# Windowed attention and a gated FFN: the first FFN products tile by tile, q and k transposed on TensorE up to tile 12, five load buffers and twelve V tiles

## The chip, the cores and the metric

The kernel runs on one core of a Trainium2 chip. Its time is device microseconds of one execution; the time before is the median of seven runs. The profiled execution is one of them, and all times inside the kernel are microseconds from the first instruction of its trace.

## The reference

Attention over a sliding window of 128 keys with a distance bias for each head, then an FFN with a SiLU gate on all tokens. Batch 8, 8 heads, 576 positions, head size 64; so 4608 tokens of width 512, and an inner width of 1536. All inputs and the output are float32.

```python
scores = q @ k.T / sqrt(64)
rel = pos[:, None] - pos[None, :]
bias = -slope[h] * abs(rel)                # slope[h] = 2 ** -(h + 1)
scores = where((rel >= 0) & (rel < 128), scores + bias, -1e9)
attn = softmax(scores)                     # its sum plus 1e-9 below
x = (attn @ v).transpose(0, 2, 1, 3).reshape(4608, 512)
g, val = x @ w_gate, x @ w_val
out = (g * sigmoid(g) * val) @ w_out
```

## The kernel before

**Tiles.** Two batches make a super-group of nine ranks: four tiles of 128 positions of each batch, and a ninth that holds the last 64 positions of both. There are 36 ranks and 36 attention units, one for each rank of queries. A unit p needs k of its rank and q of its own and the next rank; the units 3, 7 and 8 of a super-group use blocks of 128 queries and a combined mask.

**An attention unit.** GpSimd's queue loads q, k and v of a rank and casts them to float16 (`load_qk`, L174; `load_v`, L168). q and k go into `nat` buffers, four of each; v goes into a ring of `NV` = 14 tiles. q and k must be transposed: for ranks below `QK_DMA_FROM` = 9 on TensorE (`transposed`, L201), followed by a copy out of PSUM (q by VectorE at L206, k by ScalarE at L204, in the first four ranks all by VectorE); from rank 9 on by a DMA transpose that SP issues (`transpose`, L222). `scores` makes k times q on TensorE (L254, L282), exp on ScalarE (L259, L286) and the product with the distance mask on VectorE (L263, L290). `weighted` multiplies by v (L314), and VectorE divides by the sums (L316, L317). `x_transposed` turns x so that the FFN can use it: on TensorE with a ScalarE copy (L340, L341), from unit 24 on by DMA.

**The FFN.** Tokens form nine blocks of 512 columns; the ninth block collects the eight odd tiles of 64. `gate_val` makes, for each of the twelve row groups m, the gate product and the value product (`wide`, L363: four matmuls of 128 x 512 each), tanh on ScalarE (L374), `uu` on VectorE (L376) and `hT` on VectorE (L380). Block 0 and block 8 are multiplied by w_out in a plain way (`project`, L393); blocks 1 to 7 with seven products of half size in Strassen's manner (`strassen`, L472 to L502), whose steps are put between the next block's products at the places in `AT`.

**The first four units.** `first_tiles` runs them before the FFN, in an order written out by hand. TensorE starts with `WARM` = 7 matmuls on zeros. `REPEAT` says how often each early transpose is done, so that TensorE has something to do; only the last writes what is used. `need[i]` is the number of transposes that unit i wants. After unit 3's weighted product, the products of m = 0, 1 and 2 of block 0 are made for 384 columns (three tiles), and `wide` keeps the half-filled bank in `early`; `gate_val` adds the last 128 columns when tile 3 is transposed.

**PSUM.** `ps_f` has three banks "gv" and one "po"; `ps_a` has four banks "a" that scores, transposes and others take in turn. `OTHER` names the products of block 0 that use an "a" bank instead of a "gv" bank.

**The order.** In `first_tiles` and in the first `ALONE` = 8 half steps of the FFN (that is, m = 0 to 3), TensorE, VectorE and ScalarE keep the order of the code. After that a planner orders each engine's queue, with priorities from the order in which the code is written; SP's and GpSimd's queues are the planner's from the start. The main loop advances attention by a target that grows with the FFN's steps. `ahead` writes DMA transposes up to four units before they are needed, but stops at the first rank below `QK_DMA_FROM`. `loads_to(i + 7)` keeps the loads seven ranks ahead. Every engine works through its queue in order.

**Weights.** `load_w` brings column slices of the gate and value weights: 128 columns of each, then the next 384, then twice 512, between the loads of q, k and v. w_out comes in two halves after tile 8.

Of the kernel before, what the change touches and what calls it, by code (L numbers as in the profile page):

```python
# [15 lines left out]

P = 128
WIN = 128
QK_DMA_FROM = 9
X_DMA_FROM = 24  # L20
ALONE = 8
MANUAL = "compute"
# [1 line left out]
ENGINES = {"all": None, "compute": {ET.PE, ET.DVE, ET.Activation}, "pe": {ET.PE}}  # L24
WARM = 7
IDLE = {("k", 0): 0, ("q", 0): 2}
REPEAT = {("q", 1): 4, ("k", 1): 4, ("q", 2): 3}
FIRST = 4
LEAD = 6
PRE = 0  # L30
# [4 lines left out]
def slot(h):  # L35

    return 4 * (h // 4) + 2 * (h % 2) + (h % 4) // 2
# [9 lines left out]
def kernel(  # L47
# [10 lines left out]
    nc = tc.nc  # L58
# [21 lines left out]
    idm = consts.tile([P, P], FP16, name="idm")  # L80
    nc.scalar.dma_start(idm, idm_d.ap())

    idm2 = consts.tile([P, P], FP16, name="idm2")
# [14 lines left out]
    idle = kT[:, NK - 1].rearrange("p j t -> p (j t)")  # L98
# [19 lines left out]
    wv2 = moe_w_val.rearrange("(kb p) f -> p kb f", p=P)  # L118
    wo2 = moe_w_out.rearrange("(a p) d -> p a d", p=P)

    nat = ctx.enter_context(tc.tile_pool(name="nat", bufs=4))
    epool = ctx.enter_context(tc.tile_pool(name="ep", bufs=3))
    xpool = ctx.enter_context(tc.tile_pool(name="xp", bufs=3))
    bpool = ctx.enter_context(tc.tile_pool(name="bp", bufs=3))
# [9 lines left out]
        for _ in range(n):  # L134
            nc.tensor.matmul(t_, idle[:, 0:P], idle, start=True, stop=True)

    NV = 14
    va_all = []
    for n in range(NV // 2):
        tv = consts.tile([P, 2, H, D + 1], FP16, name=f"va{n}")  # L140
# [15 lines left out]
    def source(src, rank):  # L156

        s, c = divmod(rank, 9)
        if c == 8:
            return [((64 * n, 64 * n + 64),  # L160
                     src[2 * s + n, :, 512:576, :].rearrange("h p d -> p h d")) for n in range(2)]
        b, t = 2 * s + c // 4, c % 4
        return [((0, P), src[b, :, t * P:(t + 1) * P, :].rearrange("h p d -> p h d"))]

    def load_v(rank):
        va[rank] = va_all[rank % NV]
        for (p0, p1), src in source(v, rank):
            nc.gpsimd.dma_start(va[rank][p0:p1, :, 0:D], src)  # L168
# [8 lines left out]
    def load(rank):  # L177
        load_qk(rank)
        load_v(rank)

    def transposed(name, rank):

        if rank < FIRST:
            pt = ps_f.tile([P, 4, P], FP32 if (name, rank) in hw else FP16, name="pt",
                           tag="gv" if name == "k" else "po", bufs=3 if name == "k" else 1)
        else:
            pt = ps_a.tile([P, 4, P], FP16, name="pt", tag="a")
        if (name, rank) in hw:

            for _ in range(IDLE[(name, rank)]):  # L190
                nc.tensor.matmul(pt.rearrange("p j t -> p (j t)"), idle[:, 0:P], idle,
                                 start=True, stop=True)
            for j in range(4):
                nc.tensor.transpose(pt[:, j, :], hw[(name, rank)][:, j * P:(j + 1) * P], idf)
            nc.vector.tensor_copy(transposed_home(name, rank), pt)
            return
        t_ = (natk if name == "k" else natq).pop(rank)

        for _ in range(REPEAT.get((name, rank), 2) if rank < FIRST else 1):
            for j in range(4):  # L200
                nc.tensor.transpose(pt[:, j, :], t_[:, 2 * j:2 * j + 2, :],  # L201
                                    idm if rank < FIRST else idm2)
        if name == "k" and rank >= FIRST:
            nc.scalar.copy(transposed_home(name, rank), pt)  # L204
        else:
            nc.vector.tensor_copy(transposed_home(name, rank), pt)  # L206
# [9 lines left out]
    def transpose(n):  # L216
        name, rank = order[n]
        if rank < QK_DMA_FROM:
            transposed(name, rank)
# [74 lines left out]
    def weighted(i):  # L294

        s, p = units[i]
        x = xpool.tile([P, H, D], FP16, name="x", tag="x")
        xs[i] = x
        for half in range(2):
            pool, tag = (ps_f, "gv") if i < FIRST else (ps_a, "a")  # L300
            av = pool.tile([P, 4, D + 1], FP32, name="av", tag=tag)
            todo = []
            for j in range(4):
                h = 4 * half + j
                if p == 8:
                    for n, kt in enumerate((3, 7, 8)):
                        todo.append((j, ex[(s, "c", n)][:, slot(h), :], va[9 * s + kt][:, h, :]))
                else:
                    if p not in (0, 4):
                        todo.append((j, ex[(s, p - 1)][:, slot(h), 128:256],  # L310
                                     va[9 * s + p - 1][:, h, :]))
                    todo.append((j, ex[(s, p)][:, slot(h), 0:128], va[9 * s + p][:, h, :]))
            for n, (j, w, val) in enumerate(todo):
                nc.tensor.matmul(av[:, j, :], w, val, start=(n == 0), stop=(n == len(todo) - 1))  # L314
            rec = xpool.tile([P, 4, 1], FP32, name="rec", tag="rec", bufs=4)
            nc.vector.reciprocal(rec, av[:, :, D:D + 1])  # L316
            nc.vector.tensor_mul(x[:, 4 * half:4 * half + 4, :], av[:, :, 0:D],  # L317
                                 rec.broadcast_to([P, 4, D]))
# [31 lines left out]
    hT = {}  # L350

    early = {}
    OTHER = {(0, 1, "v"), (0, 2, "g"), (0, 2, "v")}

    def wide(n, m, which, c1=512):

        w, ms = wg_sb if which == "g" else wv_sb, slice(m * P, (m + 1) * P)
        ps, c0 = early.pop((n, m, which), (None, 0))
        if ps is None:
            pool, tag = (ps_a, "a") if (n, m, which) in OTHER else (ps_f, "gv")  # L360
            ps = pool.tile([P, 512], FP32, name="p" + which, tag=tag)
        for kb in range(NKB):
            nc.tensor.matmul(ps[:, c0:c1], w[:, kb, ms], xT[n][:, kb, c0:c1],  # L363
                             start=(kb == 0 and c0 == 0), stop=(kb == NKB - 1 and c1 == 512))
        if c1 < 512:
            early[(n, m, which)] = (ps, c1)
        return ps
# [136 lines left out]

    AT = {*range(2, 9), *range(10, 17)}

    def ffn():

        for n in range(NBLK):
# [6 lines left out]
            for m in range(NMB):  # L518
                for half, _ in enumerate(gate_val(n, m)):
                    yield 1.0  # L520
                    if n > 1 and 2 * m + half in AT:
                        next(parts)
# [25 lines left out]
    def transposes_to(n):  # L548
        nonlocal done_t
        while done_t < n:  # L550
            transpose(done_t)
            done_t += 1

    def ahead(i):

        n = need[min(i + 4, last)]
        while done_t < n and order[done_t][1] < loaded and order[done_t][1] >= QK_DMA_FROM:
            transposes_to(done_t + 1)

    def run(steps):  # L560
        for fs in steps:
            for f in fs:
                f()
            yield

    def first_tiles():

        first_masks()
        transposes_to(need[0] + 1)
        for n, _ in enumerate(run(scores(0))):  # L570
            if n == 2:
                transposes_to(need[1])
        for i in range(FIRST):
            if i + 1 < FIRST:
                for n, _ in enumerate(run(scores(i + 1))):
                    if n == 0 and i + 2 < FIRST:
                        transposes_to(need[i + 2])
            weighted(i)
            if i > 0:
                x_transposed(i - 1)  # L580

        for m, which in ((0, "g"), (0, "v"), (1, "g")):
            wide(0, m, which, 384)
        x_transposed(FIRST - 1)
        for m, which in ((1, "v"), (2, "g"), (2, "v")):
            wide(0, m, which, 384)

    def attention():

# [17 lines left out]
    def load_w(c0, c1):  # L607
        for src, dst in ((wg2, wg_sb), (wv2, wv_sb)):
            nc.gpsimd.dma_start(dst[:, :, c0:c1], src[:, :, c0:c1])
# [8 lines left out]
    load_qk(3, "k")  # L618
    load_v(2)
    load_v(3)  # L620
    load_w(0, 128)
    load_w(128, 512)
    load(4)
    load_qk(5, "q")
    load_w(512, 1024)
# [29 lines left out]
    def everything():  # L655
        nonlocal done
        base = 0
        busy(WARM)
        with tc.manual_schedule(engines=ENGINES[MANUAL]):
            first_tiles()  # L660
            done = FIRST
            steps = progress(ffn())
            while (at := next(steps)) < ALONE:
                if at == 4.0:
                    make_masks()
                if at == 6.0:
                    nc.scalar.copy(idm2, idm)
        for step in steps:

            b1 = 24 + 3 * PRE  # L670

            lead = LEAD if done < X_DMA_FROM - 2 else LEAD + 4
            blk = (0 if step + LEAD < b1 else 1 if step + LEAD < 60
                   else min(NBLK - 1, 2 + int((step + lead - 60) // 34.5)))
            if step < b1:

                target = base + max(0, step - ALONE) + max(0, step - 16) * (32 - b1 + ALONE) / (b1 - 16)
            elif step < 60:
                target = base + 32 + SECOND * 8 * (step - b1) / (60 - b1)
            else:  # L680
                target = base + 32 + SECOND * 8 + (step - 60) * RATE * 8 / 34.5
            while (n_att < target or done < ready[blk]) and att_step():
                pass
# [32 lines left out]
```

## Time and profile before

| what | value |
|---|---|
| median of 7 runs | 360.1 us (358.19 to 362.95) |
| the profiled execution | 359.31 us |
| its span, first to last instruction | 357.5 us |
| TensorE busy | 340.0 us |
| VectorE busy | 271.2 us |
| ScalarE busy | 177.6 us |
| mean granted TensorE clock | 0.999 |
| DMA transposes, qT and kT | 27 and 27 |
| packets of GpSimd's DMA queue | 116224, 18.62 MB |
| packets of SP's and ScalarE's DMA queue | 43232, 18.49 MB |

The span is what lies between the first and the last instruction of the trace; the time of the same execution is 1.8 us more. In a row of a timeline the first number is the start, the second the length, then come engine, line, operation, what is written from what, the shape and the count; the bracket holds the idle time of the engine before it and what ended that. Matmuls that follow each other overlap, so that the length of a group is less than its count times the length of one. A digit in a row of slices is the busy share of one fortieth of the span (8.9 us), in tenths.

### The profile page before, as it was taken

The page shows a single profiled execution, that of the slowest core. Times are in us where ns is not written, and L with a number is a line of the kernel's source. Part 1 is how long each engine was busy: PE and PEld are TensorE (multiplying, and loading weights), DVE is VectorE, ACT ScalarE, POOL GpSimd, SP SyncE. Part 2 cuts the span into 40 slices and gives each one's busy share as a digit, 9 for nine tenths or more (in the row PEclk, how much of TensorE's full clock was granted, in tenths as well). Part 3 has the DMA queues.
Part 4 walks back from the last instruction along what each step waited for, and adds up shares of the span by engine and source line. Part 5 has one row for each costly group of instructions (what it writes and reads, how often), then busy time and mean ns, then how long its engine had stood idle before and what let it go on. Part 6 is the DMA issues. An engine that isn't in the chain of part 4 may idle for free.

```text
span 357.5 us, 7133 instructions
## 1 busy us (share of the span) xinstructions
PE 340.0 (95%) x2701; PEld 193.6 (54%) x2701; DVE 271.2 (76%) x594; ACT 177.6 (50%) x351; POOL 106.7 (30%) x132
## 2 busy tenths in 40 slices
PE   7788997999999999999999999999999999999995
PEld 4554453444456655565466655564665566456543
DVE  4748974997887699768987998789877955975540
ACT  4737684455655455556565454555454323333321
POOL 8954662574926355556420001000000000000000
PEclk9999999999999999999999999999999999999999
DMA  9999999999999999999992213202021201101104
GB/s 150 170 186 187 167 175 95 133 118 160 131 152 153 146 162 175 178 154 162 176 143 87 41 67 32 85 20 75 15 76 29 75 2 59 60 2 60 60 17 102
DMA packets 159939, 37.87 MB, mean 106 GB/s; under 512 B 150432, under 2 KB 155424, under 8 KB 159904
## 3 DMA queue, kind: packets, MB, share of 16 engines
q0 software_dynamic: 116224, 18.62, 81.5%
q1 hardware_dynamic: 43232, 18.49, 28.5%
q8 instruction: 21, 0.34, 0.4%
q10 hardware_dynamic: 448, 0.30, 0.3%
q14 instruction: 14, 0.11, 0.1%
HBM read 37.91 MB, written 9.44 MB: 132 GB/s over the span
## 4 chain that ended last, share of the span: by engine, by line
PE 69%; DMA 15%; DVE 7%; POOL 4%; ACT 3%; issue 2%; ACTq 0%; POOLq 0%; SPq 0%; DVEq 0%
PE pg L363 21%; PE pv L363 20%; PE po L472 15%; DMA wv_sb<-in_moe_w_val_dram 6%; DMA qT<-qn 3%; PE av L314 3%; PE ps L254 3%; DMA wo_sb<-in_moe_w_out_dram 3%; PE po L393 2%; DMA qn<-in_q_dram 2%; PE p L472 2%; DVE uu L376 2%; DVE hT L380 1%; POOL va L168 1%; ACT exc L286 1%
## 5 line engine op out<-in xcount | busy, mean ns | idle before, releaser
L374 ACT ACTIVATE tt<-pg 128x512 f16<-128x512 f32 x108 | 64.9, 603 | 109.6 <-PE pg L363 103.6
L363 PE MATMUL pg<-xT,wg_sb 128*128 128x512 f16 (+2 forms) x444 | 115.4, 374 | 1.0 <-ACT xT L341 0.7
L363 PE MATMUL pv<-xT,wv_sb 128*128 128x512 f16 (+2 forms) x444 | 113.1, 373 | 1.2 <-DVE uu L376 1.2
L376 DVE SCALAR_TENSOR_TENSOR uu<-tt,pg 128x512 f16<-128x512 f16 x107 | 73.0, 683 | 37.8 <-ACT tt L374 37.4
L380 DVE TENSOR_TENSOR hT<-uu,pv 128x512 f16<-128x512 f16 x108 | 73.7, 682 | 6.0 <-PE pv L363 2.7
L363 PEld LDWEIGHTS <-wg_sb 128*128 128x128 f16 x444 | 41.5, 98 | 38.0 <-issue 3.5
L363 PEld LDWEIGHTS <-wv_sb 128*128 128x128 f16 x444 | 41.2, 98 | 38.5 <-issue 4.9
L259 ACT ACTIVATE ex<-ps 128x512 f16<-128x512 f32 x96 | 50.0, 610 | 9.5 <-PE ps L254 9.4
L168 POOL DMA_DIRECT2D va<-in_v_dram x40 | 34.4, 869 | 42.7 <-PE av L314 32.2
L174 POOL DMA_DIRECT2D qn<-in_q_dram x39 | 33.8, 871 | 34.9 <-DMA qT<-qn 21.5
L174 POOL DMA_DIRECT2D kn<-in_k_dram x39 | 33.5, 865 | 29.6 <-DMA kT<-kn 24.4
L472 PEld LDWEIGHTS <-hT 128*128 128x128 f16 x336 | 32.1, 98 | 14.9 <-issue 1.2
L263 DVE TENSOR_TENSOR ex<-ex,m_reg 128x1024 f16<-128x1024 f16 x48 | 32.8, 686 | 8.5 <-ACT ex L259 8.3
L472 PEld LDWEIGHTS <-S 128*128 128x128 f16 x252 | 23.9, 98 | 12.7 <-issue 4.1
L317 DVE TENSOR_TENSOR x<-av,rec 128x256 f16<-128x256 f32 x72 | 28.6, 420 | 0.4
L286 ACT ACTIVATE exc<-psc 128x512 f16<-128x512 f32 x40 | 21.0, 604 | 5.7 <-PE psc L282 5.7
L472 PE MATMUL po<-T,hT 128*128 128x256 f16 x168 | 22.9, 272 | 0.1
L472 PE MATMUL po<-T,S 128*128 128x256 f16 x168 | 22.9, 273 | 0.0
L314 PE MATMUL av<-va,ex 128*128 128x65 f16 x384 | 20.7, 193 | 2.2 <-DVE x L317 1.3
L314 PEld LDWEIGHTS <-ex 128*128 128x128 f16 x384 | 18.1, 97 | 6.3 <-DVE x L317 2.0
L254 PE MATMUL ps<-qT,kT 64*128 64x256 f16 x192 | 18.0, 272 | 3.6 <-DMA qT<-qn 2.1
L393 PE MATMUL po<-wo_sb,hT 128*128 128x512 f16 x84 | 19.7, 379 | 0.0
(72 smaller groups left out, 278.7 us busy)
## 6 DMA issues: line engine op xcount, KB each, us to landing
out_dram<-osb SPq DMA_DIRECT2D x32, 256.0 KB, 3.0
va<-in_v_dram POOLq DMA_DIRECT2D x32, 128.0 KB, 7.9
qn<-in_q_dram POOLq DMA_DIRECT2D x31, 128.0 KB, 8.1
kn<-in_k_dram POOLq DMA_DIRECT2D x31, 128.0 KB, 8.0
wo_sb<-in_moe_w_out_dram POOLq DMA_DIRECT2D x2, 768.0 KB, 9.9
wg_sb<-in_moe_w_gate_dram POOLq DMA_DIRECT2D x2, 512.0 KB, 10.6
wv_sb<-in_moe_w_val_dram POOLq DMA_DIRECT2D x2, 512.0 KB, 12.3
out_dram<-osb SPq DMA_DIRECT2D x6, 128.0 KB, 2.3
```

The lines of the kernel that those rows point to most:

```text
L168: nc.gpsimd.dma_start(va[rank][p0:p1, :, 0:D], src)
L174: nc.gpsimd.dma_start(t_[p0:p1], src)
L254: nc.tensor.matmul(two[par][:, j, :], kT[rows, ks, pair, :], qT[rows, p:p + 2, pair, :], start=(j == 0), stop=(j == 1))
L259: nc.scalar.activation(e[:, o:o + 2, :], banks[q4][par], AF.Exp, scale=scale)
L263: nc.vector.tensor_mul(e[:, o, :], e[:, o, :], reg[:, o, :])
L314: nc.tensor.matmul(av[:, j, :], w, val, start=(n == 0), stop=(n == len(todo) - 1))
L317: nc.vector.tensor_mul(x[:, 4 * half:4 * half + 4, :], av[:, :, 0:D], rec.broadcast_to([P, 4, D]))
L363: nc.tensor.matmul(ps[:, c0:c1], w[:, kb, ms], xT[n][:, kb, c0:c1], start=(kb == 0 and c0 == 0), stop=(kb == NKB - 1 and c1 == 512))
L374: nc.scalar.activation(tt, pg, AF.Tanh, scale=0.5)
L376: nc.vector.scalar_tensor_tensor(out=uu, in0=tt, scalar=one if (n, m) == PIN else 1.0, in1=pg, op0=ALU.add, op1=ALU.mult)
L380: nc.vector.tensor_mul(hT[n][:, m, :], uu, pv)
L472: nc.tensor.matmul(dst, a[:, m, cols], b[:, m, :], start=(start and m == 0), stop=(m == HM - 1), skip_group_check=True)
```

## The change

- `QK_DMA_FROM` goes from 9 to 13: q and k of ranks 9 to 12 are transposed on TensorE, with the copies that belong to it.
- `nat` has five buffers for q and five for k instead of four; the ring of V has twelve tiles instead of fourteen.
- The first slice of the gate and value weights is 256 columns instead of 128, the second 256 instead of 384.
- `begin` makes products of block 0 for the tiles that are there: those of m = 0 and 1 for one tile in unit 2 and for the second in unit 3; those of m = 2 for two tiles after that; then the third tile for all. `OTHER` now names the four products of m = 0 and 1, so those of m = 2 use "gv" banks.
- In the units 1 to 3 each half of `weighted` begins with two matmuls of 256 columns on zeros.
- `REPEAT`: k of rank 1 two instead of four times, q of rank 2 four instead of three times. q of rank 2 is transposed one step earlier in the code, ahead of unit 0's mask products.
- The copy of the identity (`idm2`) and the four mask copies move to other half steps of the FFN, and the steps of Strassen's products to other places in `AT` (the same number of places).

```diff
--- before.py
+++ after.py
@@ -16,7 +16,7 @@
 
 P = 128
 WIN = 128
-QK_DMA_FROM = 9
+QK_DMA_FROM = 13
 X_DMA_FROM = 24
 ALONE = 8
 MANUAL = "compute"
@@ -24,7 +24,7 @@
 ENGINES = {"all": None, "compute": {ET.PE, ET.DVE, ET.Activation}, "pe": {ET.PE}}
 WARM = 7
 IDLE = {("k", 0): 0, ("q", 0): 2}
-REPEAT = {("q", 1): 4, ("k", 1): 4, ("q", 2): 3}
+REPEAT = {("q", 1): 4, ("k", 1): 2, ("q", 2): 4}
 FIRST = 4
 LEAD = 6
 PRE = 0
@@ -118,7 +118,7 @@
     wv2 = moe_w_val.rearrange("(kb p) f -> p kb f", p=P)
     wo2 = moe_w_out.rearrange("(a p) d -> p a d", p=P)
 
-    nat = ctx.enter_context(tc.tile_pool(name="nat", bufs=4))
+    nat = ctx.enter_context(tc.tile_pool(name="nat", bufs=5))
     epool = ctx.enter_context(tc.tile_pool(name="ep", bufs=3))
     xpool = ctx.enter_context(tc.tile_pool(name="xp", bufs=3))
     bpool = ctx.enter_context(tc.tile_pool(name="bp", bufs=3))
@@ -134,7 +134,7 @@
         for _ in range(n):
             nc.tensor.matmul(t_, idle[:, 0:P], idle, start=True, stop=True)
 
-    NV = 14
+    NV = 12
     va_all = []
     for n in range(NV // 2):
         tv = consts.tile([P, 2, H, D + 1], FP16, name=f"va{n}")
@@ -299,6 +299,11 @@
         for half in range(2):
             pool, tag = (ps_f, "gv") if i < FIRST else (ps_a, "a")
             av = pool.tile([P, 4, D + 1], FP32, name="av", tag=tag)
+            if 0 < i < FIRST:
+
+                for _ in range(2):
+                    nc.tensor.matmul(av.rearrange("p j d -> p (j d)")[:, 0:256], idle[:, 0:P],
+                                     idle[:, 0:256], start=True, stop=True)
             todo = []
             for j in range(4):
                 h = 4 * half + j
@@ -350,7 +355,7 @@
     hT = {}
 
     early = {}
-    OTHER = {(0, 1, "v"), (0, 2, "g"), (0, 2, "v")}
+    OTHER = {(0, 0, "g"), (0, 0, "v"), (0, 1, "g"), (0, 1, "v")}
 
     def wide(n, m, which, c1=512):
 
@@ -504,7 +509,7 @@
 
 
 
-    AT = {*range(2, 9), *range(10, 17)}
+    AT = {2, 3, *range(5, 10), *range(11, 18)}
 
     def ffn():
 
@@ -563,12 +568,18 @@
                 f()
             yield
 
+    def begin(n, tiles):
+
+        for m, which in ((0, "g"), (0, "v"), (1, "g"), (1, "v"), (2, "g"), (2, "v"))[:n]:
+            if early.get((0, m, which), (None, 0))[1] < tiles * P:
+                wide(0, m, which, tiles * P)
+
     def first_tiles():
 
         first_masks()
         transposes_to(need[0] + 1)
         for n, _ in enumerate(run(scores(0))):
-            if n == 2:
+            if n == 0:
                 transposes_to(need[1])
         for i in range(FIRST):
             if i + 1 < FIRST:
@@ -576,14 +587,15 @@
                     if n == 0 and i + 2 < FIRST:
                         transposes_to(need[i + 2])
             weighted(i)
+
+            if i >= 2:
+                begin(4, i - 1)
             if i > 0:
                 x_transposed(i - 1)
-
-        for m, which in ((0, "g"), (0, "v"), (1, "g")):
-            wide(0, m, which, 384)
+        begin(6, 2)
+        begin(4, 3)
         x_transposed(FIRST - 1)
-        for m, which in ((1, "v"), (2, "g"), (2, "v")):
-            wide(0, m, which, 384)
+        begin(6, 3)
 
     def attention():
 
@@ -618,8 +630,8 @@
     load_qk(3, "k")
     load_v(2)
     load_v(3)
-    load_w(0, 128)
-    load_w(128, 512)
+    load_w(0, 256)
+    load_w(256, 512)
     load(4)
     load_qk(5, "q")
     load_w(512, 1024)
@@ -661,10 +673,10 @@
             done = FIRST
             steps = progress(ffn())
             while (at := next(steps)) < ALONE:
-                if at == 4.0:
+                if at == 2.0:
+                    nc.scalar.copy(idm2, idm)
+                if at == 5.0:
                     make_masks()
-                if at == 6.0:
-                    nc.scalar.copy(idm2, idm)
         for step in steps:
 
             b1 = 24 + 3 * PRE
```

## The prediction

> **What bounds the kernel.** I read the page first: busy shares, then the slices.
>
> ```profile
> PE 340.0 (95%) x2701; PEld 193.6 (54%) x2701; DVE 271.2 (76%) x594; ACT 177.6 (50%) x351; POOL 106.7 (30%) x132
> PE   7788997999999999999999999999999999999995
> PEclk9999999999999999999999999999999999999999
> DMA  9999999999999999999992213202021201101104
> ```
>
> TensorE is busy 340.0 of 357.5 us, its clock is full in every slice, and its free time lies in the first seven slices (some 62 us) and the last. So the next view is TensorE's timeline for those 62 us. In each row the bracket is the idle time before the work and what ended it:
>
> ```profile
> 11.85 0.61 PE L254 MATMUL ps<-qT,kT 64*128 64x256 f16 x8 [1.24 <-DVE qT L206]
> ...
> 21.57 0.81 PE L363 MATMUL pg<-xT,wg_sb 128*128 128x384 f16 x4 [0.67 <-ACT xT L341]
> ...
> 25.69 0.39 PE L363 MATMUL pg<-xT,wg_sb 128*128 128x128 f16 x4
> ...
> 30.35 0.38 PE L201 MATMUL pt<-idm,kn 128*128 128x128 f16 x4
> 30.57 0.61 PE L201 MATMUL pt<-idm,qn 128*128 128x128 f16 x8
> 32.14 1.02 PE L363 MATMUL pv<-xT,wv_sb 128*128 128x512 f16 x4 [0.96 <-DVE uu L376]
> ...
> 60.90 0.27 PE L254 MATMUL ps<-qT,kT 64*128 64x256 f16 x1 [2.06 <-DMA qT<-qn]
> ```
>
> Adding the idle rows from 11.85 to 60.90 gives 8.1 us; after 61 us the idle rows over 0.15 us add to only 2.2. After 61 us, then, an instruction added to TensorE costs its full time, and a faster other engine brings nothing. Before 61 us, VectorE's and the loads' timelines say what TensorE waits for:
>
> ```profile
> 10.76 0.69 DVE L263 TENSOR_TENSOR ex<-ex,m_reg 128x1024 f16<-128x1024 f16 x1 [1.01 <-ACT ex L259]
> 11.37 0.42 DVE L206 COPY qT<-pt 128x512 f16<-128x512 f16 x1
> ...
> 48.30 0.88 POOL L174 DMA_DIRECT2D qn<-in_q_dram  x1
> 49.20 2.62 POOL L168 DMA_DIRECT2D va<-in_v_dram  x3
> 60.41 0.88 POOL L174 DMA_DIRECT2D qn<-in_q_dram  x1 [8.59 <-DMA kT<-kn]
> ```
>
> From 13.2 to 20 us the windows view gives VectorE 6.61 busy of 6.80: it is the bound there. The last fence shows GpSimd's load queue standing 8.59 us behind a DMA transpose. Over the span the DMA slices say 9 at 95 GB/s around there (slice 6 of the page) against 175 a slice earlier: the transposes fill the DMA engines without moving much.
>
> **Start to 13 us.** k of tile 1 is transposed twice instead of four times, q of tile 2 four times instead of three. A 128-column transpose takes 219 ns alone, but four end within 0.38 us, so one more costs 0.056. Eight fewer take 0.45 us off before tile 0's products (at 9.22), which then wait for the copy of q1 (ends 8.85): 0.3 gained. That copy of q2 (L206) is now ahead of the first mask product in VectorE's order. Products 8.9 to 9.45, sixteen transposes of 1.06 us (the row at 7.34), copy 10.5 to 10.9, and tile 1's products start at 10.95 instead of 11.85. VectorE's chain from 13 us on hangs on these, so it moves 0.9 us earlier and its last weighted tile ends near 20.75 instead of 21.64.
>
> **FFN products in slices.** Before, the six products of m = 0 to 2 wait until three tiles are there (21.57), and their last 128 columns start at 25.69. After, four of them take tiles 0 and 1 into the gaps of the weighted stage. From VectorE at 20.75: the transposes of tile 2's x sit behind the second slice (16 matmuls, 0.88 us), so they start near 20.8; start to copied xT took 1.2 us (20.31 to 21.51), so xT is there at 22.0; third slices 0.88, tile 3's transposes at 22.9, its xT at 24.0, with m = 2's slices between. Last columns from 24.0: **1.7 us earlier**. The twelve extra matmuls on zeros (256 columns, half of the 0.217 spacing of the 512 rows: 1.3 us) stand where TensorE waits for VectorE; without that cover they would cost 1.3, and I take 0.
>
> A rule speaks against slicing. The Trainium skill, "TensorE: Matmul & The Clock Gate", section "Back-to-back issue gap", gives about 81 ns per matmul of 128 columns in a stream of weight loads and matmuls. Eighty such and eight of 256 columns would be 7.3 us; by the rows here (0.056 and 0.108) 5.3, against 5.25 for the 24 of 384 (0.162) and 24 of 128 before. By the page the slices lose 2 us and eat the gain; the rows of this trace cover the same shape with its weight loads, so I take 0.1.
>
> **Halved W slices.** The first pieces, 128 columns, were issued at 10.05 and 10.79 and landed 5.3 and 5.0 us later; the 384-column ones, issued at 11.52 and 12.25, landed at 18.6 and 20.5, 1.9 us apart for 384 KB. Two of 256 KB first should land near 16.1 and 17.4. They are wanted at about 17.8, so a wait lies between 0 and 0.5; I take 0. The total bytes are unchanged.
>
> **Banks of m = 2 to 4.** m = 2's products now take two of the three "gv" banks, so m3's value product waits for the uu of m2. VectorE's series of uu and hT, 0.6 us apart, starts 1.7 us earlier (25.0), so m2's uu ends near 28.1; TensorE stands from 26.2 to 28.1. Then come m3's value product, twelve transposes (0.66), and m4: its value product starts near 30.6 against 32.14. So the 0.96 us wait goes, one of 1.9 comes instead, and **1.5 to 1.6** of the lead is left. The mask copies move behind m2's tanh (2.3 us on ScalarE), hidden by VectorE's series; the idm2 copy (0.3) too.
>
> **Five load buffers.** At 38.23 tile 8's k load waits 0.39 us for a k buffer, and wo's first half goes ahead of it. With five it can go first; wo's piece took 3.0 us of landing (44.2 to 47.2), so tile 8 lands up to 3 us earlier. That lets the lead survive to 58.8 us, where block 0's output products end. If not, the lead waits for tile 8's data (nearest 0, at most 1.6 lost). Twelve V tiles instead of fourteen: V of tile 12 goes out at 50.9 onto tile 0's place, free since 15 us; later ones are early by tens of us. I take 0.
>
> **Tiles 9 to 12 on TensorE.** Eight transposes times four matmuls times 0.056 is **1.8 us** added, and 8 copies (four of 0.59 on ScalarE, four of 0.42 on VectorE, which has 2.9 us free of 20 between 60 and 80): hidden, up to 1.7 if VectorE has no room. Removed: the **2.06 us** wait at 60.90. q of tile 10 landed at 56.4 (48.30 + 8.1), its DMA transpose only at 60.8. By TensorE it is ready at 56.4 + 0.22 + 0.42 and some 0.3 of handing over, 57.3; TensorE gets there at 58.84 - 1.6 + three transposes 0.66, about 57.9. So the wait goes whole. The Trainium skill speaks against moving transposes here too (same page, "Part 4: PE-mode transpose"): about 275 ns each in one kernel. 32 of them would be 8.8 us, and the change would lose 5; the rows (0.38 for four, running on from each other) make it 1.8, and they decide.
>
> The moved Strassen places (one slot later) change no count; the four waits of 0.3 to 0.4 on L476 may move: within 0.5 either way, 0 taken.
>
> **Sum.** -1.6 - 2.06 + 1.8 = -1.9 us. The profiled execution took 359.31 (span 357.5 and 1.8 around it), so 357.4; it lies 0.8 below the median of 360.1, so the median becomes **358.2**. A measurement of this kernel can tell about 1% (3.6 us) from no change.
>
> **Rivals.** (a) *The wait moves.* DMA transposes now begin at tile 13, and only after tile 12's are written, so its k and q get one tile of lead; the old rank-9 wait (2.06) can reappear near 92 us, where tile 13 follows tile 12 within 3 us. Or tile 8's data holds the early lead back. Either takes about 2: 360.3. For: the DMA slices stay at 9. Against: the load queue no longer stands 8.6 us behind transposes.
> (b) *More of the idle time goes.* If the new bank wait doesn't come (VectorE ahead) and the waits for x at 43 to 54 us go (0.7), and those at 27.48 (0.29) and 37.75 (0.26): 1.7 + 1.25 + 0.26 + 0.7 + 2.06 - 1.8 = 4.2, median 355.9. The end of this: all 8.1 idle gone less 1.8 and 1.3, -5.0, 355.1.
> (c) *Slower: TensorE stops at loads.* TensorE takes its queue in order. A DMA transpose waiting for a load holds SP; one on TensorE holds every FFN product behind it. Loads there took 8.1 to 9.5 us to land. If the transposes of tiles 10, 11 and 12 stand 2 us or more ahead of their loads, that is 6 + 1.8 with only 2.06 and 1.6 back: +4.1, 364.2. It decides once these waits pass 5.5 us together. For: 37.75 already shows 0.26 us of this on q. Against: the transposes of tiles 4 to 8 had no other.
>
> **Chances.** Forecast 0.42 (own range 356.4 to 359.8), (a) 0.15, (b) 0.27, (c) 0.16. Faster by over 1%: (b) and a rim of the forecast, 0.30; slower: (c), 0.16; the rest 0.54. Range: from (b)'s end, 355.1, to 362.8, into (c).
>
> **What would show it.** Tile 1's products near 10.95; last 128 columns of m = 0 near 24.0; a wait of 1.9 us on uu before m3's value product; tile 9's scores near 58 with no wait on qT; 32 more TensorE transposes under L201 and 46 DMA transposes instead of 54; after 61 us TensorE idle still near 2 us. Wrong, if rows of L201 wait on qn or kn for over 1 us each, or if idle time after 61 us exceeds 4 us.

## The result, and the profile after

The changed kernel takes **357.85 us** (median of 26 runs, 357.63 to 358.07); the kernel before took 359.36 in the runs beside it (63 runs, 358.1 to 362.95). The ratio is 0.9952, 95% interval 0.9939 to 0.9966: 0.5% faster, within the 1% that the prediction set as its bound. The forecast was 358.2. The profiled executions took 359.31 and 357.88, with spans of 357.5 and 356.1 us. Fastest against fastest, 358.1 and 357.63, the difference is only 0.5 us; the rest of the 1.5 between the medians comes from the spread of the kernel before, which the changed one does not have. Its profiled execution is one near the median; no trace of a fast one was kept.

The page of the changed kernel, in the same rows as before:

```profile
PE 342.4 (96%) x2781; PEld 197.9 (56%) x2781; DVE 274.3 (77%) x597; ACT 179.6 (50%) x355; POOL 106.7 (30%) x132
PE   7898899999999999999999999999999999999995
PEclk9999999999999999999999999999999999999999
DMA  9999999999999999999995413312021201101014
```

TensorE now does 2.4 us more and the span is 1.4 shorter. The added work and the removed waits both show at once; where they lie is in TensorE's timeline of the changed kernel:

```profile
10.99 0.77 PE L254 MATMUL ps<-qT,kT 64*128 64x256 f16 x8 [0.52 <-DVE qT L206]
...
24.12 0.38 PE L368 MATMUL pg<-xT,wg_sb 128*128 128x128 f16 x4 [0.23 <-ACT xT L346]
...
28.84 1.04 PE L368 MATMUL pv<-xT,wv_sb 128*128 128x512 f16 x4 [1.15 <-DVE uu L381]
...
31.43 1.04 PE L368 MATMUL pv<-xT,wv_sb 128*128 128x512 f16 x4
...
36.11 0.39 PE L201 MATMUL pt<-idm,kn 128*128 128x128 f16 x4
37.64 0.40 PE L201 MATMUL pt<-idm,qn 128*128 128x128 f16 x4 [1.14 <-DMA qn<-in_q_dram]
37.87 1.03 PE L368 MATMUL pg<-xT,wg_sb 128*128 128x512 f16 x4
...
57.20 0.81 PE L398 MATMUL po<-wo_sb,hT 128*128 128x512 f16 x3
57.85 0.22 PE L201 MATMUL pt<-idm,kn 128*128 128x128 f16 x1
58.04 1.02 PE L368 MATMUL pg<-xT,wg_sb 128*128 128x512 f16 x4
```

Some rows of the kernel before at the same places:

```profile
37.10 0.39 PE L201 MATMUL pt<-idm,kn 128*128 128x128 f16 x4
37.75 0.40 PE L201 MATMUL pt<-idm,qn 128*128 128x128 f16 x4 [0.26 <-DMA qn<-in_q_dram]
...
58.02 0.81 PE L393 MATMUL po<-wo_sb,hT 128*128 128x512 f16 x3
...
61.10 1.04 PE L363 MATMUL pg<-xT,wg_sb 128*128 128x512 f16 x4
```

Laid side by side, they show how the lead runs:

| work on TensorE | before | after | lead |
|---|---|---|---|
| tile 1's scores | 11.85 | 10.99 | 0.86 |
| last 128 columns, m = 0 | 25.69 | 24.12 | 1.57 |
| m4's value product | 32.14 | 31.43 | 0.71, with a tile's scores (0.55) now ahead of it |
| k of tile 6 transposed | 37.10 | 36.11 | 0.99 |
| q of tile 6 transposed | 37.75 | 37.64 | 0.11 |
| block 0's last output products | 58.02 | 57.20 | 0.82 |
| block 1's first product | 61.10 | 58.04 | 3.06 |
| end of the span | 357.5 | 356.1 | 1.4 |

The lead is made by 24 us. Some 0.6 of it is gone by 36.11, and 0.88 more is lost at 37.64 in one wait on a load: the FFN product behind it in TensorE's queue, which doesn't use that q, starts only at 37.87. The lead comes back in part because three waits for x between 43 and 55 us (0.72 together before) are gone, and grows by the 2.06 us wait at 60.90, which is gone too. The other 31 matmuls of the new transposes come after 58.04: 31 x 0.056 = 1.7 us, and 3.06 - 1.7 leaves the 1.4 of the end. The idle rows over 0.15 us after 61 us add to 2.2 before and 2.0 after.

### The profile page after: what moved, and what is told of

Its sections match the earlier page's. It is cut to its first block, busy times and chain, and to the rows that moved or that the text cites. A ratio compares the mean times of both kernels' runs of the same rounds, so it can differ in the third digit from the quotient of the medians.

```text
span 356.1 us, 7266 instructions
## 1 busy us (share of the span) xinstructions
PE 342.4 (96%) x2781; PEld 197.9 (56%) x2781; DVE 274.3 (77%) x597; ACT 179.6 (50%) x355; POOL 106.7 (30%) x132
## 4 chain that ended last, share of the span: by engine, by line
PE 74%; DVE 13%; ACT 6%; DMA 4%; issue 2%; POOL 0%; DVEq 0%; ACTq 0%
PE pg L368 21%; PE pv L368 21%; PE po L477 14%; PE av L319 4%; DMA qn<-in_q_dram 4%; PE ps L254 3%; PE po L398 3%; DVE uu L381 2%; DVE hT L385 2%; PE p L477 2%; DVE ex L263 2%; PE px L345 2%; ACT ex L259 2%; ACT exc L286 2%; ACT tt L379 1%
## 5 line engine op out<-in xcount | busy, mean ns | idle before, releaser
L368 PE MATMUL pv<-xT,wv_sb 128*128 128x512 f16 (+2 forms) x464 | 115.1, 365 | 1.6 <-DVE uu L381 1.6
L368 PEld LDWEIGHTS <-wv_sb 128*128 128x128 f16 x464 | 42.5, 98 | 38.9 <-issue 3.7
L368 PEld LDWEIGHTS <-wg_sb 128*128 128x128 f16 x464 | 42.5, 98 | 35.1 <-issue 2.3
L346 ACT COPY xT<-px 128x512 f16<-128x512 f16 x24 | 14.1, 586 | 15.0 <-PE px L345 15.0
```

## The experiments

The experiments stand in three sets, each on another chip and with runs of the kernel before beside it. That kernel's medians in the three sets were 358.55, 359.15 and 358.77, so a difference below some 0.4 us between sets is not read. A ratio is given with its 95% interval; it is not the quotient of the two medians and can lie nearer to 1. "Granted clock" is that of single executions, over the whole span. In the profiled executions a value of 0.994 or 0.995 goes with 3.4 us at half clock, which costs the mean 0.005, and 0.990 with 6.8 us; so 0.995 or less is read as a stretch of half clock in the others too.

### The early part alone

REPEAT, the order of q2, `begin`, `OTHER`, the matmuls on zeros, the W slices and the places of the mask copies; all else as before.

```diff
 (the changed kernel)
-QK_DMA_FROM = 13
+QK_DMA_FROM = 9
-name="nat", bufs=5
+name="nat", bufs=4
-NV = 12
+NV = 14
-AT = {2, 3, *range(5, 10), *range(11, 18)}
+AT = {*range(2, 9), *range(10, 17)}
```

> Only the early part of the change: REPEAT, q2 ahead of the mask products, begin, OTHER, the matmuls on zeros, the W slices and the places of the mask copies; loads, V ring, transposes and AT as before. My theory: the lead of 1.6 us at 24 us is lost at 37.6 us, where q of tile 6 lands, so 0 to 0.4 us are left: 359.0 to 359.4. Rival, that the lead lasts to the end: 1.2 to 1.6 less than before, 357.8 to 358.2.

Measured: 362.14 us against 358.55, ratio 1.008 (1.0048 to 1.0111). **Slower**, which neither theory had. TensorE's timeline, SP's row of the DMA transpose that it waits for, and then the windows view (length, busy time of TensorE, weight loads, VectorE, ScalarE, GpSimd with their counts, granted clock, DMA share, GB/s):

```profile
61.83 0.37 PE L254 MATMUL ps<-qT,kT 64*128 64x256 f16 x1 [4.14 <-DMA qT<-qn]
```

```profile
57.60 1.21 SPq L222 DMA_TRANSPOSE qT<-qn  x1
```

```profile
58.00:62.00 4.00, 0.17 (x1) 0.10 (x1) 0.00 (x0) 0.32 (x1) 0.66 (x1) 0.92 1.13 91
62.00:66.00 4.00, 4.00 (x13) 1.53 (x13) 1.23 (x2) 0.60 (x1) 4.00 (x6) 0.65 1.16 74
```

The wait for the transposed q of tile 10 is 2.08 us longer than before, for two reasons. TensorE is there 1.15 earlier (57.69 against 58.84), so its lead turns into waiting; and the data come 0.93 later (61.83 against 60.90). The same row of SP stands at 56.46 in the kernel before: q of tile 10 was asked for earlier here (45.70 against 48.30) but took 11.6 us to land instead of 8.1, with both halves of w_out issued closely ahead of it (40.49 and 42.27; 37.02 and 43.08 before). And during so long a wait the clock was halved: 0.65 in the window after it, with TensorE busy all 4.00 us. All twelve executions had a granted clock of 0.991 to 0.995. At 37 us this run waited for q of tile 6 only 0.19 us, since it started 0.65 later (7.94 against 7.29 at the first tile); my theory's place was not tested by it, and the outcome that it named was wrong.

### Only the transposes of tiles 9 to 12 back on DMA

```diff
 (the changed kernel)
-QK_DMA_FROM = 13
+QK_DMA_FROM = 9
```

> The changed kernel with q and k of tiles 9 to 12 transposed by DMA again. My theory: the wait for the transposed q of tile 10 near 59 us comes back with 2 us or more, and 32 TensorE transposes (1.8 us) go; a median of 358.2 to 358.8 (the changed kernel has 357.85). Rival, that the gain is the early lead and this part only breaks even: 357.6 to 358.0, with no wait over 0.5 us near 59.

Measured: 362.46 against 358.55, ratio 1.0073 (1.004 to 1.0106). The theory had the wait but not its size:

```profile
62.52 0.37 PE L254 MATMUL ps<-qT,kT 64*128 64x256 f16 x1 [4.54 <-DMA qT<-qn]
```

```profile
58.13 1.19 SPq L222 DMA_TRANSPOSE kT<-kn  x1
59.43 3.01 SPq L222 DMA_TRANSPOSE qT<-qn  x2
```

```profile
58.00:62.00 4.00, 0.00 (x0) 0.00 (x0) 0.00 (x0) 0.60 (x1) 0.53 (x1) 0.79 1.47 140
62.00:66.00 4.00, 3.48 (x9) 1.30 (x10) 0.62 (x1) 0.60 (x1) 4.00 (x6) 0.50 1.36 110
66.00:70.00 4.00, 4.00 (x21) 1.63 (x20) 3.22 (x7) 1.14 (x3) 2.47 (x3) 0.86 2.34 140
```

Half the clock lasts from 60.3 to 67.1 in this trace. With all other edits in place, moving these eight transposes to TensorE is worth some 4.6 us (362.46 to 357.85), though 1.8 us of TensorE time is paid for it. Nearly half of that is the wait alone: the two executions at full clock took 359.78 and 360.01, the nine with a lower clock 361.8 to 362.9. The five buffers don't help here. The loads are late: k and q of tile 10 took 12.4 and 12.2 us to land (until 58.1 and 58.8), and q's transpose also stands behind k's in SP's queue.

### The late part alone, and with the zeros

The kernel before with DMA transposes from tile 13, five buffers, twelve V tiles and the new `AT`:

> Only the late part: DMA transposes from tile 13, five load buffers, twelve V tiles, the new AT; the first four tiles and the W slices as before. My theory: nearly the whole gain, 1.1 to 1.5 us: 357.9 to 358.3. Rival (the gain is the early lead): 0.2 to 0.4 less than before, 359.0 to 359.2.

Measured: 359.58 against 358.55, ratio 1.001 (0.9981 to 1.0039): no gain, so my theory fell, and the rival was right that this part does no more than break even. But the executions fall in two groups: five at full clock, 358.4 to 358.9, and seven with a granted clock of 0.989 to 0.995, 359.5 to 361.5. The profiled one is of the second; the windows view:

```profile
14.00:18.00 4.00, 2.95 (x52) 1.92 (x48) 3.90 (x11) 3.45 (x8) 4.00 (x6) 1.00 1.42 194
18.00:22.00 4.00, 2.58 (x35) 1.59 (x36) 3.37 (x12) 1.60 (x3) 2.05 (x4) 0.95 2.15 165
22.00:30.00 8.00, 7.71 (x56) 4.69 (x55) 1.57 (x3) 2.90 (x6) 4.33 (x6) 0.81 1.55 194
```

From 21.6 to 25.0 us the clock is half, and no wait in the 8 us ahead of it is longer than 0.77 us; TensorE is busy for 2.95 and 2.58 of 4 us in the first two windows. That alone does not bring the clock down: the profiled execution of the kernel before did nearly the same work there, 3.05 and 2.47 of 4 us, at full clock.

```profile
14.00:18.00 4.00, 3.05 (x52) 2.01 (x52) 3.90 (x11) 3.45 (x8) 3.93 (x5) 1.00 1.44 198
18.00:22.00 4.00, 2.47 (x35) 1.60 (x36) 3.48 (x12) 1.70 (x4) 2.17 (x4) 1.00 2.18 164
```

The timeline of the late part alone shows the price, four matmuls of 384 columns in 1.35 instead of 0.81 us:

```profile
21.46 1.35 PE L363 MATMUL pg<-xT,wg_sb 128*128 128x384 f16 x4 [0.67 <-ACT xT L341]
```

So the same kernel was run with the matmuls on zeros:

```diff
 (the late part alone)
+            if 0 < i < FIRST:
+                for _ in range(2):
+                    nc.tensor.matmul(av.rearrange("p j d -> p (j d)")[:, 0:256], idle[:, 0:P],
+                                     idle[:, 0:256], start=True, stop=True)
             todo = []
```

> The late part alone, with the matmuls on zeros put into units 1 to 3. Theory: the late part breaks even at full clock (2.06 less of waiting, 1.8 more of transposes), and its 359.58 held a half-clock stretch in more than half of its executions; with the zeros the clock stays full: 358.3 to 358.9, all executions within 0.8. Rival, that the late part itself costs 1 us: the zeros change nothing, 359.3 to 359.9.

Measured: 358.65 (358.37 to 358.96) against 359.15, ratio 0.9988 (0.997 to 1.0006), no execution below a clock of 0.998. As the theory had it: the late part breaks even, and the zeros hold the clock (none of twelve executions with a low clock, where it was seven of twelve without them, on another chip). The windows view of its profile:

```profile
14.00:18.00 4.00, 3.59 (x58) 2.62 (x58) 3.90 (x11) 3.23 (x7) 4.00 (x5) 1.00 1.44 198
18.00:22.00 4.00, 2.77 (x43) 2.09 (x42) 3.51 (x12) 1.94 (x4) 1.94 (x4) 1.00 2.17 165
```

The changed kernel beside it took 357.71, so the rest of the early part is worth 0.94 once the late part is there.

### Without the zeros

```diff
 (the changed kernel)
-            if 0 < i < FIRST:
-                for _ in range(2): ...
```

> The changed kernel without the matmuls on zeros in units 1 to 3. Theory now: they keep the clock. Without them some executions grant half the clock for one stretch of 3.4 us around 20 us, as in the late part alone, and lose 1.7 us; executions between 357.6 and 359.6, in two groups, median 357.7 to 359.3. Rival, that the FFN products in the gaps are enough and the matmuls on zeros only delay VectorE's chain (0.2 to 0.4 us): one group, 357.4 to 357.8.

Measured: 358.0 (357.54 to 358.93) against 357.71 for the changed kernel, one of twelve executions at a clock of 0.995. The difference lies outside the span: the twelve spans, 355.8 to 356.2, are those of the changed kernel (355.7 to 356.3), that of the execution with the low clock too. So it is the rival in the main: the slices in the gaps do nearly all of the work of keeping the clock, and the zeros neither cost nor gain anything that shows at the end. Early on they do cost: the last 128 columns of m = 0 start at 23.79 without them and at 24.12 with them. In the changed kernel TensorE is busy through the place where the clock fell in the late part alone:

```profile
18.00:22.00 4.00, 4.00 (x76) 3.89 (x74) 2.93 (x10) 1.15 (x3) 3.01 (x4) 1.00 2.21 164
```

### The zeros in the kernel before

> The kernel before with the matmuls on zeros in units 1 to 3 and nothing else. Theory: they keep the clock near 20 us, so the executions with a half-clock stretch there go; but the wait at 60.9 stays, and with it what it does to the clock. 358.1 to 358.9, against 358.6 to 359.4 for the kernel before. Rival, that the spread of the kernel before is all from the wait at 60.9: no change.

Measured: 360.9 against 358.77, ratio 1.004 (1.0012 to 1.0068). Slower, which I hadn't expected. In its profile the transposed q of tile 10 arrives later, since its DMA transpose took 5.3 us to land instead of 4.3:

```profile
61.67 0.27 PE L254 MATMUL ps<-qT,kT 64*128 64x256 f16 x1 [2.99 <-DMA qT<-qn]
```

And ten of its twelve executions had a clock of 0.995 or less. The profiled one had 0.998, so no trace shows where the others lost it; the place is open, and so is whether the zeros delay that transpose or only this execution has it late.

### One number: transposes from tile 13

```diff
 (the kernel before)
-QK_DMA_FROM = 9
+QK_DMA_FROM = 13
```

> The kernel before with one number changed: DMA transposes from tile 13. Theory: 2.06 us of waiting go and 1.8 us of transposes come, so 0 to 0.4 less than before at equal clock, with the half-clock stretches of the first 25 us still there: a median within 0.6 of the kernel before. Rival, that the five buffers are what takes the wait away: the wait near 60 stays on a load, and the time is 1.5 to 2 us over before.

Measured: 359.55 against 358.77, ratio 1.0005 (0.9975 to 1.0035); the medians differ by 0.78, a little more than the 0.6 that I had allowed. No wait is left near 60 us:

```profile
58.50 0.22 PE L201 MATMUL pt<-idm,kn 128*128 128x128 f16 x1
58.69 1.02 PE L363 MATMUL pg<-xT,wg_sb 128*128 128x512 f16 x4
```

With four buffers the wait is gone as well, so the rival is out. Five executions at full clock took 358.25 to 358.53, seven with half-clock stretches 359.5 to 361.3. The seven full-clock executions of the kernel before beside it spread over 358.29 to 360.34. So this one number takes away the spread that does not come with the clock, but hardly any time from the fastest executions.

### Four buffers and fourteen V tiles

```diff
 (the changed kernel)
-name="nat", bufs=5
+name="nat", bufs=4
-NV = 12
+NV = 14
```

> The changed kernel with four load buffers and fourteen V tiles, as before; transposes on TensorE up to tile 12. Theory: without the fifth buffer the loads of tiles 9 to 12 go out behind buffers that are still held and tile 8 behind half of wo; a wait on a load of 0.5 to 2 us comes near 48 or 60, 358.3 to 359.8. Rival, that the transposes on TensorE alone free the buffers in time: 357.5 to 358.0.

Measured: 357.82 (357.51 to 358.03), beside 357.71 and 357.85 for the changed kernel in its two other sets of runs. The rival was right: the fifth buffer and the smaller ring are worth nothing; no wait on a load came but the known one (0.90 at 37.67).

### Tile 6 ahead of the last W slice

The changed kernel's wait of 1.14 us at 37.64 ends when q of tile 6 lands. Its load goes out at 24.47, and the DMA view of that moment gives its time to landing:

```profile
24.47 0.88 POOL L174 DMA_DIRECT2D qn<-in_q_dram  x1
```

```profile
qn<-in_q_dram POOLq DMA_DIRECT2D x1, 128.0 KB, 13.1
```

13.1 us, because the last two W pieces (512 KB each) are ahead of it in the queue; with the order changed it took 9.8 from an issue at 22.71. This is the change of places:

```diff
 (the changed kernel)
-    load_w(1024, 1536)
     load(6)
+    load_w(1024, 1536)
     load(7)
```

> The changed kernel with tile 6's q, k and v loaded ahead of the last W slice instead of behind it. My theory: q of tile 6 lands some 5 us earlier, the 1.14 us wait at 37.64 goes and the lead reaches the end: 0.9 to 1.2 less than the changed kernel, 356.6 to 357.0, if the last W slice (2.9 us later) is still there before m = 8 wants it near 39. Rival, that VectorE's chain or tile 8's data bounds the stretch up to 58 us anyway: the wait goes and others come between 38 and 58, no gain, 357.6 to 358.0.

> The changed kernel once more, beside the next one on one chip: 357.6 to 358.1, clock full in every execution.

> The changed kernel with tile 6 loaded ahead of the last W slice, once more. Theory: the wait for q of tile 6 (1.14 us) was the lead's loss, so 1.0 to 1.2 less than the changed kernel beside it, 356.5 to 357.0. Rival, that the chips differ: within 0.3 of it.

Measured: 356.74 in the first set (one of its twelve executions took 360.06 at full clock, which no trace explains); in the second 356.65 (356.42 to 356.85) beside 357.71 for the changed kernel: **1.06 us less**, as expected. TensorE's timeline of this kernel in the second set has the same transposes without a wait, at 36.05 and 36.28:

```profile
36.05 0.39 PE L201 MATMUL pt<-idm,kn 128*128 128x128 f16 x4
36.28 0.39 PE L201 MATMUL pt<-idm,qn 128*128 128x128 f16 x4
```

Nearly the whole wait reaches the end of the kernel, so nothing else bounds the stretch from 38 to 58 us by as much.

### That, with DMA transposes from tile 11

```diff
 (tile 6 ahead of the last W slice)
-QK_DMA_FROM = 13
+QK_DMA_FROM = 11
```

> The changed kernel with tile 6 ahead of the last W slice and DMA transposes from tile 11 instead of 13. Theory: 16 fewer TensorE transposes at 0.056 each, 0.9 us less than the kernel with tile 6 first (356.7): 355.6 to 356.0, if the transposed q of tile 11 lands before 73 us, where it is wanted. Rival, that the loads of tile 11 land near 66 and its transposes behind others: a wait of over 1 us on qT near 70, 356.8 to 358.5.

Measured: 356.0 (355.9 to 356.28) against 358.77, ratio 0.9897 (0.9858 to 0.9936): the fastest kernel of this study, below both of the pair. Against 356.65 and 356.74 for tile 13 in the other sets, 16 fewer matmuls are worth 0.65 to 0.74; 0.9 was reckoned. No wait on qT came; one for x at 84.20 takes 0.40 where it took 0.18.

## Why the prediction was right

The total was right (358.2 forecast, 357.85 measured), and the steps were partly so. That the forecast came so near is luck in part: from one profiled execution to the other the gain was 1.43 instead of 1.9, and the 0.8 by which the median of seven stood above the profiled execution, and which was added to the forecast, is nothing in the changed kernel (357.85 against 357.88). Two misses of 0.5 and 0.8 nearly cancel.

- **Start to 13 us**: right. 10.95 reckoned, 10.99 measured.
- **FFN products in slices**: right. Last columns from 24.0 reckoned, 24.12 measured; the first W pieces were reckoned at 16.1 and 17.4, and landed at 15.6 and 17.7 (10.04 + 5.6, 10.78 + 6.9). The rows of 0.056 per 128 columns held, and not the 81 ns that the Trainium skill gives ("TensorE: Matmul & The Clock Gate", "Back-to-back issue gap"): in the changed kernel groups of four such matmuls start 0.22 to 0.23 apart (18.14, 18.36, 18.59). The loss of 2 us by that page was over-reckoned, since its 81 ns were put against a sum of before that has 0.056; with 81 ns on both sides it is 1.5. VectorE's last weighted tile ended at 21.1, not 20.75. The zeros, taken as 0, cost 0.33 here (23.79 without them).
- **Banks of m = 2 to 4**: the wait for uu came, but 0.21 and 1.15 instead of 1.9, because the planner put the twelve transposes of tiles 4 and 5 into it (26.32 to 27.5), where I had them behind it. That brought a copy of q into VectorE's series ahead of m2's uu, which ended at 28.78 instead of 28.1:

```profile
27.18 0.42 DVE L206 COPY qT<-pt 128x512 f16<-128x512 f16 x1
27.51 0.68 DVE L385 TENSOR_TENSOR hT<-uu,pv 128x512 f16<-128x512 f16 x1
28.10 0.68 DVE L381 SCALAR_TENSOR_TENSOR uu<-tt,pg 128x512 f16<-128x512 f16 x1
```

Of the 1.5 to 1.6 that should be left, 1.26 was (0.71 and the scores of 0.55), and 0.99 at 36.11.
- **Five load buffers**: this step failed. It let the lead survive to 58.8 us, and if anything were to hold it, tile 8's data. Tile 6's q held it, 21 us before that: in the kernel before, its row at 37.75 already showed a wait of 0.26 us on the load, so a lead at this point turns into waiting unless the load comes earlier too; it came only 0.1 earlier. I had that row, counted it as 0.26 of idle time to be gained and as a hint for (c), and not as the place where the lead ends. The buffers themselves do nothing, as the run with four shows.
- **Tiles 9 to 12 on TensorE**: the sum of this step was right, -2.06 + 1.8, and the late part with a full clock does break even (358.65 against 359.15 in one set, 358.4 to 358.9 against a median of 358.46 for the kernel before's full-clock executions in another). Tile 9's scores did not come near 58 but at 65.4; the planner put block 1's products first, which costs nothing. What the step missed is what it protects: without it, the lead of the early part turns into a longer wait and a halved clock, 362.1 to 362.5. The parts don't add.
- **Rivals**: the slice at 95 GB/s, read as transposes that fill the DMA engines, is in part one without loads: from 60 to 62 us their share was 0.11, at 20 GB/s. (a) happened in its second form at another tile, and took 0.9 of the lead; of (b) the waits for x went, 0.7. The two nearly cancel, so the span's gain held better than the steps. (c) did not happen: the one wait of an L201 row on a load in the stretch that it names is that of tile 6, which was on TensorE before. By its length, 1.14 us, it is still one of the rows set as a sign of being wrong, and what it showed wrong is the step of the load buffers.
- **The clock** was taken as full from the profile's page. In the changed kernel it is: none of its 39 executions had 0.995 or less. Of the kernel before's 94 in the three sets of experiments, 59 did. Yet its full-clock executions are only about 0.3 us faster in two of the sets and no faster in the third, and spread over some 2 to 2.7 us themselves. That early lost time is later absorbed by the wait at 60.90 would explain the first, and that this wait differs from execution to execution the second; both are argued and not shown, since the one trace of that kernel is of an execution with the full clock. So how much of the gain between the medians is the wait that every execution had, and how much its long cases, stays open. In the two kernels without that wait and without the zeros (late part alone, and one number), a low clock costs 1.2 and 1.5 us between the medians of the two groups.

## What to carry to other kernels

A lead made early is worth only what the next fixed arrival lets through: before counting it, follow the engine's rows downstream and mark each one that already waits for a load or a transfer, however short that wait is, for there the lead can end. Such a row also says what to do, here to change the order of two loads. And where an engine's clock depends on its work, test parts together: one that shortens work can lengthen a wait until the clock falls, as the early part alone did here, and the sum of the parts says nothing then.

## What the runs showed of the hardware

- TensorE's half clock came in stretches of 3.4 us or twice that: 21.6 to 25.0 in the late part alone, 61.35 to 64.8 in the early part alone, 60.3 to 67.1 with tiles 9 to 12 on DMA. In the profiled executions with waits of 4.14 and 4.54 us it came within the wait, 3.7 and 2.3 us after TensorE's last matmul; with a wait of 2.99 us (zeros in the kernel before) it did not come. The Trainium skill, "TensorE: Matmul & The Clock Gate", Part 1, has the clock halved after an idle window of about 3.4 us, in windows that run freely. The lengths of the stretches fit that; but the stretch at 21.6 came with TensorE busy for 2.58 of 4 us and no gap over 0.77, and that at 60.3 after only 2.3 us of idle time, so here a whole idle window was not needed.
- The same work can have the full clock or not: seven of twelve executions of the late part alone had a low one and five had not.
- A profile of one execution can show a full clock in every slice where most executions of the same kernel don't have it.
- The changed kernel's times lie within 0.44 us, those of the kernel before within 4.9. With only the transposes of tiles 9 to 12 moved, the full-clock executions lie within 0.3 us, and the rest of the spread is that of the clock.
- A DMA transpose of one tile landed 4.3 to 6.1 us after its issue beside loads at 53 to 57 us (kernel before), and 2.4 to 2.5 us at 69 to 71 us in the changed kernel, where the DMA engines' share was 0.15 to 0.43.
